# Hashed attention with a two-layer tail: later hashes and first maxima for three heads, and the maxima of a step ahead of the normalisation

## The chip, the cores and the metric

The program runs on one core of a Trainium2 chip. The metric is the device time of one execution in microseconds (us). Five engines work beside each other, each in its own order: TensorE (PE in the profile; its weight loads are PEld), VectorE (DVE), ScalarE (ACT), GpSimd (POOL) and SyncE (SP), whose queue issues most of the DMAs.

## The reference, cut to what matters

Attention with a hash mask, over 2 batches of 8 heads, 768 positions and 64 dimensions. A mixture-of-experts layer and a second two-layer network follow; the change touches only the attention.

```python
q_bits = (np.einsum('bhsd,dk->bhsk', q, proj) > 0)      # 6 bits: the bucket of a position
mask = q_bucket[:, :, :, None] == k_bucket[:, :, None, :]
scores = scale * np.matmul(q, k.transpose(0, 1, 3, 2))
scores = np.where(mask, scores, -1000000000.0)
scores = scores - np.max(scores, axis=-1, keepdims=True)
attn = np.exp(scores)
attn = attn / (np.sum(attn, axis=-1, keepdims=True) + 1e-09)
return np.matmul(attn, v)
```

## The kernel before

The 16 heads (batches laid end to end) are cut into 96 units of 128 keys, six to a head. The loop over `s` (line 950) issues one unit's scores in each step, and everything else at fixed offsets from it. The string `ORDER` (line 38) gives the order in which the parts of one step are issued; an engine runs its instructions in that order. The letters are:

- `a`, `b`: `ST(s, 0)` and `ST(s, 1)`, the scores of unit `s` against the two halves of the queries (two matmuls each, lines 861 and 862), and the exponential by ScalarE (L863).
- `V`: `vsplit(h, 0)`, ScalarE's scaled copy of a head's values (L755); its second half, two VectorE instructions (L759, L760), is issued at `o`.
- `D`: `flush()`, which issues the DMAs that the step before put off: hash rows into the operand slots (`op<-big`, L650), the slots' other parts (`op<-A`, `op<-B`, L650), loads, flags.
- `N`: `NORM(h)`, issued at steps 10, 16, 22 and so on: three VectorE instructions (L888 to L890) that read the accumulator `av` of head `h`.
- `m`, `n`: `MAX(u, 0)` and `MAX(u, 1)` for the units `us` of this step: a matmul of row block `u` of a head against half the keys (L829), and a VectorE maximum over it (L830). The hash rows must be in the slot before.
- `e`: `EL(s-1)`, the split of the exponentials into two float16 parts (L867 on ScalarE, L868 on GpSimd).
- `p`: `POSTa`, after the last unit of a head, joins the halves (L832). One step later `POSTb` is issued at `L`: a transpose on TensorE (L835), two VectorE instructions (L837, L841) and DMAs that put the maxima of the head into its slot (L838).
- `A`: in every second step `AV(s-5)` and `AV(s-4)`, 18 matmuls each into `av` (L876 to L878); for a head's last unit six more (L882). There is one `av` buffer, so a head's first `AV`, one step after `NORM`, must wait for `NORM` of the head before.
- `L`: `slot`, whatever `PLAN` (line 40) puts at the end of a step: `Z(...)`, hash matmuls (L802 to L804) with a threshold on VectorE (L809), `T(...)`, conversions and DMAs, `vscale` and `vscale2` (L734 to L749), `vtot`.

`ps5` gives `ST` and `MAX` five PSUM buffers in turn; all short work shares the two `misc` buffers. The first maxima (units 0 to 5) are taken ahead of the loop. How far the maxima run ahead is set by `us` (line 951): at most `cap[s]` units in step `s` (2 where the list has ended), and never past unit `s+10`. With the list of before, the maxima of head 2 (units 12 to 17) fall into steps 4, 4, 5, 5, 6 and 7, those of head 3 into steps 8 to 13, those of head 4 into steps 14 to 19. `Z3=(4,5)` puts the two halves of head 3's hash matmuls into steps 4 and 5.

Of the kernel before, what the change touches and what calls it, by code (L numbers as in the profile page):

```python
# [34 lines left out]
PB = 1  # L35
LAGS = (0, 0)
HB = 3
ORDER = "aVDNmbnefopAL"
PM = 2
PLAN = dict(  # L40
    v0=(1, 3, 4), T3=(2, 2), Z3=(4, 5), T=(2, 4, 5, 7), Z=(8, 10), ld=0, am1=(4, 6, 8, 9), am=(4, 6, 8,
    10), sc=(13, 15), tot=3, tot0=6, sp=(-2, 4, 10, 18), cap=(3, 2, 0, 1), x=(1, 2, 7, 3), x3=(0, 1, 2, 2), x4=(9, 10, 13, 11), w1=(91, 92, 95, 96, 97, 98, 99, 100), ga=(87, 88, 90), vl=1, am0=(0, 0), Z2=(0, 1), x6=(0, 1, 6, 4), first=(57, 58, 59, 60, 66, 72, 75, 78, 83, 84, 85, 86),
)
NPRE = 3
NT = 22
# [458 lines left out]
def _program(base, tc, nc, q, k, v, proj, mod, w_gate, mbias, w1, w2, win, wout, alpha, out):  # L504
# [445 lines left out]
    for s in range(96+LAG+2):  # L950
        us=[u for u in range(nu,min(96,s+6+LA+1,nu+(PLAN["cap"][s] if s<len(PLAN["cap"]) else 2)))]; nu+=len(us)
        fs=dq[:]; dq.clear()
        for o in "aVDNbmnefopAL" if s==0 else ORDER:
            t=s-1-LAG
# [613 lines left out]
```

## Time and profile before

| | us |
|---|---|
| median of three runs | 685.57 (683.86 to 687.6) |
| the profiled execution, its own time | 686.88 |
| its span, first to last instruction | 685.1 |
| PE busy | 656.4 (96%) |
| VectorE busy | 446.7 (65%) |
| ScalarE busy | 315.3 (46%) |
| GpSimd busy | 236.0 (34%) |

The span is that of the profiled execution, and all times of rows are counted from its start. The attention takes about the first 250 us. A matmul's record reaches to its modelled end, and matmuls overlap, so the idle time printed behind a row is a better guide to a wait than the busy share.

### The profile page before, as it was taken

Reading aid. Unit: us, or ns where it says so; the run is one execution under the profiler, and the core shown is the slowest. Engines: PE = TensorE matmul, PEld = TensorE weight load, DVE = VectorE, ACT = ScalarE, POOL = GpSimd, SP = SyncE. Lnnn points to the kernel's source line nnn. Section 1 sums busy time; section 2 is a strip of 40 time slices with the busy share of each in tenths; the row PEclk is TensorE's granted clock in tenths of the full one; section 3 lists DMA queues with packets and bytes.
Section 4 is the critical chain, followed back from the end, with each engine's and each line's share of the span. In section 5 each row is a group of like instructions: output and inputs, shape, how many; then the busy total and the mean of one; then the engine's idle time right before and its main releaser. Section 6 shows DMA issues by size and latency. Waiting matters only on the chain.

```text
span 685.1 us, 12778 instructions
## 1 busy us (share of the span) xinstructions
PE 656.4 (96%) x4938; PEld 556.2 (81%) x4938; DVE 446.7 (65%) x927; ACT 315.3 (46%) x536; POOL 236.0 (34%) x211
## 2 busy tenths in 40 slices
PE   7789999999999988999999999999999999999995
PEld 6578898998788878898888987888888888888884
DVE  6887878788888778455735668999443444433332
ACT  5567788887787843033423256665211111111111
POOL 8767999987967501310000202040030000200002
PEclk9979999999999999999999999999999999999998
DMA  8466864866603139385320834441020000100001
GB/s 217 129 146 142 187 154 97 185 185 138 140 11 125 49 107 395 119 321 201 108 61 11 285 120 154 131 146 62 1 93 1 15 16 0 47 16 0 1 0 61
DMA packets 32859, 75.02 MB, mean 110 GB/s; under 512 B 7276, under 2 KB 7366, under 8 KB 32534
## 3 DMA queue, kind: packets, MB, share of 16 engines
q1 hardware_dynamic: 29700, 64.43, 33.0%
q0 software_dynamic: 2960, 9.70, 4.3%
q8 instruction: 39, 0.64, 0.4%
q14 instruction: 30, 0.25, 0.1%
q10 hardware_dynamic: 130, 0.00, 0.0%
HBM read 49.79 MB, written 14.68 MB: 94 GB/s over the span
## 4 chain that ended last, share of the span: by engine, by line
PE 54%; DVE 1%; ACT 1%; issue 1%; POOL 1%; ACTq 0%; POOLq 0%
PE o L1413 19%; PE h L1387 18%; PE y L1074 8%; PE g L1054 8%; PE tr L1257 1%; POOL out_dram L1430 1%; PE tr L1041 0%; DVE w L1232 0%; DVE op L1232 0%; ACT op L1230 0%; DVE gl L620 0%; ACT gf L1391 0%; ACT q L1392 0%; ACT w L1230 0%; DVE big L1197 0%
## 5 line engine op out<-in xcount | busy, mean ns | idle before, releaser
L868 POOL TENSOR_TENSOR El<-E,Eh 128x768 f16<-128x768 f32 x87 | 142.7, 1652 | 36.6 <-ACT Eh L867 22.7
L863 ACT ACTIVATE E<-st 128x384 f32<-128x384 f32 x192 | 89.2, 494 | 53.3 <-PE st L862 49.8
L830 DVE TENSOR_REDUCE mx<-mxp 128x1 f32<-128x384 f32 x192 | 97.6, 548 | 9.2 <-PE mxp L829 8.7
L617 ACT ACTIVATE gh<-gf 128x512 fp32r<-128x512 f32 x48 | 30.3, 631 | 142.7 <-PE o L1413 132.2
L867 ACT ACTIVATE Eh<-E 128x768 f16<-128x768 f32 x94 | 79.8, 849 | 0.0
L861 PE MATMUL st<-op 97*128 97x384 f32 x192 | 72.9, 380 | 1.6 <-DMA op<-mr 1.3
L829 PE MATMUL mxp<-op 76*128 76x384 f32 x192 | 65.9, 357 | 7.3 <-ACT E L863 2.5
L620 DVE TENSOR_TENSOR gl<-gf,gh 128x512 fp32r<-128x512 f32 x48 | 33.1, 690 | 59.2 <-ACT gh L617 57.2
L1430 POOL DMA_INDIRECT out_dram<-x,did x12 | 11.8, 984 | 167.8 <-DVE x L1427 89.1
L1387 PE MATMUL h<-big,op 128*128 128x512 f32 x256 | 67.9, 393 | 0.0
L862 PE MATMUL st<-op 128*128 128x384 f32 x192 | 65.8, 343 | 0.0
L1413 PE MATMUL o<-op,gh 128*128 128x512 f32 x192 | 64.2, 395 | 0.0
L1245 POOL DMA_INDIRECT yg<-ys,dpos x10 | 12.3, 1231 | 138.3 <-DVE x L1197 72.8
L876 PE MATMUL av<-vh,Eh 128*128 128x65 f16 x576 | 58.5, 196 | 1.3 <-DVE big L890 1.3
L876 PEld LDWEIGHTS <-Eh 128*128 128x128 f16 x576 | 52.5, 98 | 8.4 <-issue 6.2
L1074 PE MATMUL y<-op,hh 128*128 128x512 f32 x172 | 58.6, 399 | 0.0
L877 PE MATMUL av<-vl,Eh 128*128 128x64 f16 x576 | 58.0, 194 | 0.0
L878 PE MATMUL av<-vh,El 128*128 128x65 f16 x576 | 57.8, 195 | 0.0
L1387 PEld LDWEIGHTS h<-big,op 128*128 128x128 f32 x256 | 48.1, 188 | 10.9
L877 PEld LDWEIGHTS <-Eh 128*128 128x128 f16 x576 | 53.2, 99 | 0.0
L878 PEld LDWEIGHTS <-El 128*128 128x128 f16 x576 | 53.1, 98 | 0.0
L1395 DVE TENSOR_SCALAR gf<-h,al 128x512 f32<-128x512 f32 x33 | 24.8, 751 | 41.7 <-PE h L1387 41.7
(424 smaller groups left out, 1483.2 us busy)
## 6 DMA issues: line engine op xcount, KB each, us to landing
r<-in_moe_w_dram SPq DMA_DIRECT2D x14, 1024.0 KB
op<-B SPq DMA_DIRECT2D x32, 192.0 KB
op<-A SPq DMA_DIRECT2D x28, 192.0 KB
op<-A SPq DMA_DIRECT2D x13, 384.0 KB
ys<-zero SPq DMA_DIRECT2D x19, 256.0 KB
op<-in_moe_w_in_dram SPq DMA_DIRECT2D x4, 1024.0 KB
op<-in_moe_w_out_dram SPq DMA_DIRECT2D x4, 1024.0 KB
ys<-ysb SPq DMA_DIRECT2D x13, 256.0 KB
```

Of the source, the lines that this page charges most:

```text
L829: mm(p[:,0:384],t[0:76,2,c*128:(c+1)*128],t[0:76,1,a*384:a*384+384],start=True,stop=True)
L830: nc.vector.tensor_reduce(out=mx[h][:,c,a:a+1],in_=p[:,0:384],axis=AX.X,op=ALU.max)
L861: mm(p[:,0:384],t[0:97,1,js],t[0:97,2,qs],start=True,stop=False)
L863: nc.scalar.activation(E[s][0][:,qs],p[:,0:384],AF.Exp,scale=0.125)
L867: else: nc.scalar.activation(eh,e,AF.Copy)
L868: (nc.vector if s>=ELD else nc.gpsimd).tensor_tensor(out=el,in0=e,in1=eh,op=ALU.subtract)
L876: mm(a[:,c*65:c*65+65],eh[:,cs],VH[h//4%2][:,j,h%4,:],start=(j==0 and c==0),stop=False,skip_group_check=True)
L877: mm(a[:,c*65:c*65+64],eh[:,cs],VL[h//4%2][:,j,h%4,:],start=False,stop=False,skip_group_check=True)
L878: mm(a[:,c*65:c*65+65],el[:,cs],VH[h//4%2][:,j,h%4,:],start=False,stop=False,skip_group_check=True)
L1074: nc.tensor.matmul(yps[key][i], a[:, ts], w[:, c], start=(c == 0 and m == 0), stop=(c == 7 and m == 2))
L1387: nc.tensor.matmul(p, terms[t][0][:, kk, cs], terms[t][1][:, kk], start=(n == 0), stop=(n == 11))
L1413: nc.tensor.matmul(po[b][i], a[:, ts], w[:, c % 2], start=(c == 0 and n == 0), stop=(c == 15 and n == 2))
```

## The change

Three settings. In `ORDER` the letter `N` moves from ahead of `m`, `b` to behind `n`: the three instructions of `NORM` are issued behind all maxima of their step. `Z3` becomes `(5,5)`: the first half of head 3's hash matmuls goes from step 4 to step 5. The list `cap` is longer and now sets the limits of steps 4 to 14 as well: the maxima of head 2 fall into steps 5, 5, 6, 6, 7 and 7, those of head 3 into steps 9, 9, 10, 11, 12 and 13, the first two of head 4 both into step 15; from there on all is as before. No instruction is added or taken away. Step 0 keeps an order of its own, written out in the loop.

```diff
-ORDER = "aVDNmbnefopAL"
+ORDER = "aVDmbnNefopAL"
 PLAN = dict(
-    v0=(1, 3, 4), T3=(2, 2), Z3=(4, 5), T=(2, 4, 5, 7), ...
-    10), sc=(13, 15), tot=3, tot0=6, sp=(-2, 4, 10, 18), cap=(3, 2, 0, 1), ...
+    v0=(1, 3, 4), T3=(2, 2), Z3=(5, 5), T=(2, 4, 5, 7), ...
+    10), sc=(13, 15), tot=3, tot0=6, sp=(-2, 4, 10, 18), cap=(3, 2, 0, 1, 0, 2, 2, 2, 0, 2, 1, 1, 1, 1, 0), ...
```

## Rows read from the trace of the kernel before

**Rows 1.** The page: PE's busy line; granted clock in 40 slices, tenths.
```profile
PE 656.4 (96%) x4938; PEld 556.2 (81%) x4938; DVE 446.7 (65%) x927; ACT 315.3 (46%) x536; POOL 236.0 (34%) x211
PEclk9979999999999999999999999999999999999998
```

**Rows 2.** Windows: stretch, length, busy us of each engine (instructions), granted clock, DMA share, GB/s.
```profile
30.00:50.00 20.00, 15.99 (x136) 13.06 (x135) 15.18 (x40) 12.72 (x24) 13.72 (x9) 0.74 0.51 119
50.00:160.00 110.00, 107.88 (x1495) 97.51 (x1494) 90.15 (x234) 88.44 (x164) 99.78 (x81) 1.00 0.70 163
```

**Rows 3.** Timeline of PE: start us, us, line, tile, count [idle before, releaser].
```profile
31.98 0.40 PE L747 MATMUL misc<-dg,one 128*128 128x4 f32 x2 [1.54 <-DVE dg L743]
...
33.88 0.98 PE L829 MATMUL mxp<-op 76*128 76x384 f32 x2 [0.66 <-ACT E L863]
...
38.08 0.37 PE L835 MATMUL misc<-ident,mt 128*6 128x128 f32 x1 [0.98 <-DVE vl L760]
```

**Rows 4.** Windows of one us where the granted clock falls and rises.
```profile
32.00:33.00 1.00, 1.00 (x4) 0.71 (x4) 0.97 (x4) 0.37 (x1) 1.00 (x1) 0.61 0.38 61
...
42.00:43.00 1.00, 1.00 (x21) 0.86 (x19) 0.00 (x0) 0.00 (x0) 1.00 (x1) 0.77 0.14 41
```

**Rows 5.** Timeline of SP's queue: hash rows of heads 2, 3, and 4 with 5.
```profile
30.67 1.55 SPq L650 DMA_DIRECT2D op<-big  x2
...
44.07 1.61 SPq L650 DMA_DIRECT2D op<-big  x2
...
59.85 3.14 SPq L650 DMA_DIRECT2D op<-big  x4
```

**Rows 6.** Timeline of PE: first maxima of head 3, step 9, first maxima of head 4.
```profile
48.28 0.41 PE L829 MATMUL mxp<-op 76*128 76x384 f32 x1 [0.83 <-ACT A L711]
...
49.10 0.42 PE L861 MATMUL st<-op 97*128 97x384 f32 x1
...
63.09 0.41 PE L829 MATMUL mxp<-op 76*128 76x384 f32 x1 [1.26 <-DMA op<-big]
```

**Rows 7.** Timeline of ACT, one row, and of DVE in steps 4 to 7.
```profile
33.64 0.58 ACT L755 ACTIVATE misc<-vr,sc 128x384 f32<-128x384 f32 x1
...
34.58 1.02 DVE L830 TENSOR_REDUCE mx<-mxp 128x1 f32<-128x384 f32 x2 [1.46 <-PE mxp L829]
...
37.38 0.56 DVE L760 TENSOR_TENSOR vl<-misc,vh 128x384 f16<-128x384 f32 x1
...
43.38 0.66 DVE L809 TENSOR_SCALAR big<-misc,tv 24x384 f32<-24x384 f32 x1 [1.63 <-PE misc L804]
...
47.87 0.15 DVE L832 TENSOR_REDUCE mt<-mx 128x6 f32<-128x12 f32 x1
```

**Rows 8.** Timeline of PE: the one wait of a head's first AV for NORM.
```profile
241.52 0.20 PE L876 MATMUL av<-vh,Eh 128*128 128x65 f16 x1 [1.27 <-DVE big L890]
```

**Rows 9.** Timelines of PE, then DVE: head 1's flags, next maxima, next AV, NORM.
```profile
66.24 0.36 PE L882 MATMUL av<-vt,fl 33*128 33x65 f16 x6
...
67.73 0.34 PE L829 MATMUL mxp<-op 76*128 76x384 f32 x1
...
69.11 0.21 PE L876 MATMUL av<-vh,Eh 128*128 128x65 f16 x1
...
67.02 0.21 DVE L888 TENSOR_SCALAR r<-av,sc 128x6 f32<-128x6 f32 x1
...
67.50 0.56 DVE L890 TENSOR_TENSOR big<-av,r 128x384 f32<-128x384 f32 x1
67.97 1.94 DVE L830 TENSOR_REDUCE mx<-mxp 128x1 f32<-128x384 f32 x4
```

**Rows 10.** The same for head 12, cut to the second maximum, the AV and NORM.
```profile
215.91 0.34 PE L829 MATMUL mxp<-op 76*128 76x384 f32 x1
...
217.35 0.21 PE L876 MATMUL av<-vh,Eh 128*128 128x65 f16 x1
...
215.03 0.23 DVE L888 TENSOR_SCALAR r<-av,sc 128x6 f32<-128x6 f32 x1 [0.71 <-PE av L882]
```

**Rows 11.** Timeline of PE: two later waits, for a DMA and for a maximum.
```profile
85.85 0.45 PE L861 MATMUL st<-op 97*128 97x384 f32 x1 [0.71 <-DMA op<-mr]
...
172.36 0.44 PE L829 MATMUL mxp<-op 76*128 76x384 f32 x1 [0.55 <-DVE mx L830]
```

More of the change, by code (lines that the diff above doesn't have):

```diff
@@ L37 @@
 HB = 3
-ORDER = "aVDNmbnefopAL"
+ORDER = "aVDmbnNefopAL"
 PM = 2
 PLAN = dict(
-    v0=(1, 3, 4), T3=(2, 2), Z3=(4, 5), T=(2, 4, 5, 7), Z=(8, 10), ld=0, am1=(4, 6, 8, 9), am=(4, 6, 8,
-    10), sc=(13, 15), tot=3, tot0=6, sp=(-2, 4, 10, 18), cap=(3, 2, 0, 1), x=(1, 2, 7, 3), x3=(0, 1, 2, 2), x4=(9, 10, 13, 11), w1=(91, 92, 95, 96, 97, 98, 99, 100), ga=(87, 88, 90), vl=1, am0=(0, 0), Z2=(0, 1), x6=(0, 1, 6, 4), first=(57, 58, 59, 60, 66, 72, 75, 78, 83, 84, 85, 86),
+    v0=(1, 3, 4), T3=(2, 2), Z3=(5, 5), T=(2, 4, 5, 7), Z=(8, 10), ld=0, am1=(4, 6, 8, 9), am=(4, 6, 8,
+    10), sc=(13, 15), tot=3, tot0=6, sp=(-2, 4, 10, 18), cap=(3, 2, 0, 1, 0, 2, 2, 2, 0, 2, 1, 1, 1, 1, 0), x=(1, 2, 7, 3), x3=(0, 1, 2, 2), x4=(9, 10, 13, 11), w1=(91, 92, 95, 96, 97, 98, 99, 100), ga=(87, 88, 90), vl=1, am0=(0, 0), Z2=(0, 1), x6=(0, 1, 6, 4), first=(57, 58, 59, 60, 66, 72, 75, 78, 83, 84, 85, 86),
 )
```

## The prediction

> **What bounds the kernel now.** I read the page first. PE is busy for 96% of the span, and its clock is lowest in the slice from 34 to 51 us [rows 1]. The change reaches only into the attention, so I took windows there. From 50 to 160 us PE is busy for 107.88 of 110 us: what is put on PE there, or makes it wait there, costs its full time. From 30 to 50 us it is another picture: PE 15.99 of 20, VectorE 15.18, the clock at 0.74 on average [rows 2]. Then the timeline of PE, reading only the idle time behind the rows. In steps 3 to 5 PE waits three times, 1.54, 0.66 and 0.98 us [rows 3]. The clock falls to 1.2 GHz right behind the first of these and is back at 2.4 GHz within the 43rd us: between the two lie some 10 us at half speed [rows 4]. PE had worked without a printed wait from 38.08 on when the clock rose. Two more waits stand in the change's way: 0.83 us ahead of head 3's first maximum (step 8) and 1.26 us ahead of head 4's (step 14) [rows 6].
>
> **Which of these waits the change touches.** The 1.54 us belong to step 3, where everything is issued as before; they stay, and so does the fall of the clock. The 0.66 us are put down to an exponential, but the buffer that this matmul takes (five back) held scores whose exponential was long over. What came just then are head 2's hash rows: their DMAs were issued until 32.22 [rows 5], and the matmul began 1.66 us later. Head 4's case gives the same delay: the second of four issues ends near 61.4 (half of 3.14 behind 59.85), and the matmul starts at 63.09. So this is a wait for hash rows, and one step more removes it. The 0.98 us are the wait of POSTb for a misc buffer that the value split holds until 37.94; the split stands on VectorE behind the four maxima of step 4 [rows 3, 7]. With these maxima and the first half of Z3 out of step 4, the split can start behind ScalarE's copy, at 34.25, and POSTb takes a buffer that is long free. Z3's first half goes to step 5, behind the AV matmuls, where PE does it anyway; SP's order doesn't change, since head 3's rows go out behind the second half, which stays in step 5.
>
> **Early part, placed by hand.** From 34.25 VectorE has, up to the last maximum of head 2 and its POSTa: the value splits of heads 0 and 1 (1.05 each, from the 0.56 of a row), 12 maxima (0.48 each: a pair ends after 1.02, and the rows overlap a little), two thresholds of 0.6, two absolute maxima of 0.46 and about 1 us of small ones: 2.1 + 5.8 + 1.2 + 0.9 + 1.0 = 11.0 us. It can't be through before 45.2. In the trace of before this same work ends at 48.02, because VectorE stands idle for 1.46, 1.63 us and less [rows 7]. With PE's own order laid beside it (scores of step 4 from 32.2, POSTb, step 5's scores and four maxima, AV, the six hash matmuls), VectorE waits another 0.8 us for hash and maximum matmuls if the clock is back soon, and 2.7 us if it stays low until 42.4: POSTa ends at 46.0 or at 47.9. PE is then ahead: it has done step 8's scores by 44.3 (or 46.5) and its transpose in POSTb waits for POSTa. Step 9 starts right behind, at 46.05 or 47.95 instead of 49.10 [rows 6]; it carries two more maximum matmuls than before (0.36 us). So the early part is worth 2.7 us at one end and 0.8 at the other. I take the middle, 1.8, because the rows show both an unbroken stretch of about 3.6 us behind 32.2 and a short new wait at its end (the last maximum of step 5 needs a buffer that an exponential frees near 36.5). The 0.83 us wait is inside this sum.
>
> By the Trainium skill, TensorE: Matmul & The Clock Gate, section Terms, the loss at a reduced clock is the reduced time multiplied by the missing share of the clock. By that rule the 10 us would cost 5 us, more than the whole early part gives in my sum. No row shows PE alone there; VectorE's 15.18 of 20 us [rows 2] speak against it.
>
> **Head 4's wait.** SP's hash rows for head 4 stand in a queue that runs nearly without a break from 44.07 to 63 [rows 5], and this queue starts when head 3's second threshold is through, 44.04 [rows 7], in my placement near 39.8 to 41.7. The rows land two to four us earlier, PE comes about 1.8 us earlier, and the maximum comes one step later. All of the 1.26 us goes [rows 6]. Together: 1.8 + 1.26 = 3.1 us gained.
>
> **NORM behind the maxima.** A head's first AV must wait for NORM; once before, 1.27 us [rows 8]. In heads 0 to 13 NORM is through 0.9 to 2.1 us ahead of that AV (1.05 in head 1, [rows 9]). Now two maxima (0.95 us) go ahead, and more than that where VectorE would first stand idle for the matmul of the second maximum. Head 1: the flags' matmuls have given VectorE its work at 66.24 to 66.6, NORM starts at 67.02 and ends at 68.06, AV starts at 69.11. In the new order VectorE waits for the matmul that ends at 68.07, takes that maximum from 68.12, NORM from 68.6 to 69.62: AV is late by 0.56 [rows 9]. Head 12 in the same way: matmul end 216.25, NORM 216.8 to 217.8, AV late by 0.50 instead of waiting for nothing [rows 10]. Doing this for all 13 heads that have maxima in that step gives 0.56, 0.49, 0.57, 0.26, 0.37, 0.20 and 0.50 for heads 1, 3, 5, 7, 9, 11 and 12, and 0.26 to 0.36 to spare in heads 0, 2, 4, 6, 8 and 10, which have the hash matmuls or other work between. Sum 2.95 us, on the engine that is full. Some of it can hide in later waits that don't hang on PE: head 1's 0.56 in the 0.71 us for a DMA at 85.85 [rows 11]. I take 2.4. The bounds are 3.0, or more if VectorE runs later than now (a rival), and below nothing by 0.55, since the maxima of that step come 1 us earlier and one wait for a maximum is on record [rows 11], though not in such a step.
>
> **Sum.** -1.8 - 1.26 + 2.4 = -0.7 us on the profiled execution (686.88, span 685.1), so 686.2 there. The three runs have their median 1.3 us lower, at 685.57; the forecast is 684.9. A measurement of this kernel can tell about 0.5%, 3.4 us, from no change.
>
> **Rivals.** First: the clock comes back early and PE, not VectorE, limits the early part. Then the two waits (1.64) and half of some 6.5 us at half speed (3.2) come back in full: -1.64 - 3.2 - 1.26 + 2.4 = -3.7, 681.9. For it: VectorE's idle time is of the same size. Against it: the 11.0 us of VectorE work. 0.13. By the Trainium skill's rule above the early part would go this way.
>
> Second: NORM costs nothing, because later waits like the two of [rows 11] take up the stalls (ten between 85 and 240 us, 0.2 to 0.7 each): -3.1, 682.5, or 681.0 with the early end of the first part. For it: those waits are there; against: most of the stalls lie before 160, where PE has hardly one. 0.17.
>
> Third, the slow side: VectorE is later at those steps than I place it. The point that decides is 0.3 us: from there the six heads with 0.26 to 0.36 to spare stall too. At 0.45 us later all heads lose 2.95 + 7 x 0.45 + 6 x 0.15 = 7.0 us, less 3.1: +3.9, 689.5. For it: the waits in the early part go, so PE comes to VectorE's queue sooner. Against: VectorE is busy for 90 of 110 us there [rows 2]. 0.10.
>
> **How the numbers follow.** The forecast with its bounds (gain 2.1 to 4.0, NORM -0.5 to 3.0: -4.5 to +0.9) has 0.60. The range of 681.0 to 688.6 leaves out the far end of the slow rival and the two gains added up. Faster by over 0.5% (below 682.1): the first rival, half of the second: 0.21. Slower by over 0.5% (above 689.0): most of the third: 0.08. The rest, 0.71, is no change that can be told.
>
> **What would show it.** Right: no wait at the first maxima of heads 2, 3 and 4 nor at step 4's POSTb; a new wait of PE for POSTa at step 8; step 9 starting between 46 and 48; waits of 0.2 to 0.6 us for NORM at odd heads. Wrong: a PE wait of more than 0.8 us for NORM at many heads, no such wait at any, or a second stretch at half clock near 46, which the new wait could bring on and which I have left out of the sum.

## The result: slower by 0.77%

The changed kernel takes 690.22 us in the median of seven runs (690.07 to 692.38), the kernel before 685.88 (683.86 to 687.6): a ratio of 1.0077, 95% interval 1.0059 to 1.0095. The forecast was 684.9 with a range of 681.0 to 688.6, and a chance of 0.08 that the change would cost more than 0.5%. The profiled execution took 692.38 us, its span is 690.6.

The page of the changed kernel, PE's busy line and the clock as in [rows 1]:

```profile
PE 657.6 (95%) x4938; PEld 558.4 (81%) x4938; DVE 447.5 (65%) x927; ACT 316.0 (46%) x536; POOL 236.3 (34%) x211
PEclk9998999999999989999999999999999999999999
```

The work is the same on every engine to within 1.2 us (the weight loads to within 2.2); what is new is waiting, and two slices of lower clock at other places than before. From the timeline of PE in the changed kernel, from step 3 to the end of the attention: its waits above 1.1 us, and one of its five AV waits for `NORM`:

```profile
30.34 0.39 PE L747 MATMUL misc<-dg,one 128*128 128x4 f32 x2 [1.54 <-DVE dg L743]
34.49 0.44 PE L829 MATMUL mxp<-op 76*128 76x384 f32 x1 [1.14 <-ACT E L863]
38.57 0.42 PE L861 MATMUL st<-op 97*128 97x384 f32 x1 [1.49 <-DMA op<-mr]
45.42 0.27 PE L835 MATMUL misc<-ident,mt 128*6 128x128 f32 x1 [1.40 <-DVE mt L832]
61.72 0.44 PE L829 MATMUL mxp<-op 76*128 76x384 f32 x1 [1.15 <-ACT E L863]
95.43 0.20 PE L876 MATMUL av<-vh,Eh 128*128 128x65 f16 x1 [0.63 <-DVE big L890]
...
148.85 0.73 PE L182 MATMUL misc<-ident,big 128*128 128x128 f32 x3 [1.71 <-DVE big L890]
...
245.50 0.24 PE L876 MATMUL av<-vh,Eh 128*128 128x65 f16 x1 [1.26 <-DVE big L890]
```

Step 3 is reached 1.64 us earlier than in before (30.34 against 31.98): nothing is changed ahead of it, but the clock had not fallen near 12 us in this execution (the granted clock from 12 to 13 us is 1.00, in before 0.50). So places are compared by intervals, from one head's flags' matmuls (L882) to the next. They are the start times of those rows, subtracted; the first interval begins at the L747 row of step 3.

| interval, us | before | changed | order alone | maxima alone | late at 52 only | not at 52 |
|---|---|---|---|---|---|---|
| step 3 to head 3 | 61.08 | 61.74 | 59.97 | 60.13 | 60.52 | 60.47 |
| head 3 to 7 | 52.41 | 53.46 | 53.49 | 52.43 | 52.42 | 53.48 |
| head 7 to 8 | 13.88 | 17.23 | 15.68 | 13.85 | 18.63 | 13.85 |
| head 8 to 14 | 77.21 | 77.78 | 78.17 | 77.21 | 76.78 | 78.10 |
| head 14 to 15 | 9.73 | 12.43 | 9.73 | 9.73 | 9.73 | 11.31 |

For the two profiles alone: +0.66 to head 3, +1.05 to head 7, +3.35 between heads 7 and 8, +0.57, and +2.70 in the last interval, 8.3 us; 1.64 of it was saved ahead of step 3 and 1.2 behind the attention, which leaves the 5.5 us between the spans. The +2.70 doesn't follow the change: a wait of 1.27 us stands there in before too, and the clock fell behind it in the changed kernel's execution and not in that of before. Seven of the fourteen profiles of this study have this interval at 11.0 to 12.5 us, the other seven at 9.7: five of the nine with a late normalisation, two of the five without. The +3.35 does, as the next section shows.

Over whole executions the clock is no lower than before: its mean is 0.987 in the seven runs of the changed kernel, and 0.987 in the 23 to 29 runs of the kernel before in each of the first three series below. So the change brought no more half speed in sum; its loss is waiting.

### The profile page after: what moved, and what is told of

Read it like the earlier page. It is cut to its first block, busy times and chain, and to the rows that moved or that the text cites. A ratio compares the mean times of both kernels' runs of the same rounds, so it can differ in the third digit from the quotient of the medians.

```text
span 690.6 us, 12781 instructions
## 1 busy us (share of the span) xinstructions
PE 657.6 (95%) x4938; PEld 558.4 (81%) x4938; DVE 447.5 (65%) x927; ACT 316.0 (46%) x536; POOL 236.3 (34%) x211
## 4 chain that ended last, share of the span: by engine, by line
PE 54%; DVE 1%; ACT 1%; issue 1%; POOL 1%; ACTq 0%; POOLq 0%
PE o L1413 18%; PE h L1387 18%; PE y L1074 8%; PE g L1054 8%; PE tr L1257 1%; POOL out_dram L1430 1%; PE tr L1041 0%; DVE w L1232 0%; DVE op L1232 0%; ACT op L1230 0%; DVE gl L620 0%; ACT gf L1391 0%; ACT q L1392 0%; ACT w L1230 0%; DVE big L1197 0%
## 5 line engine op out<-in xcount | busy, mean ns | idle before, releaser
L876 PE MATMUL av<-vh,Eh 128*128 128x65 f16 x576 | 60.9, 199 | 4.1 <-DVE big L890 4.1
L876 PEld LDWEIGHTS <-Eh 128*128 128x128 f16 x576 | 53.9, 100 | 11.9 <-DVE big L890 6.2
L877 PE MATMUL av<-vl,Eh 128*128 128x64 f16 x576 | 60.4, 197 | 0.0
L878 PE MATMUL av<-vh,El 128*128 128x65 f16 x576 | 60.1, 198 | 0.0
L877 PEld LDWEIGHTS <-Eh 128*128 128x128 f16 x576 | 54.6, 101 | 0.1
L878 PEld LDWEIGHTS <-El 128*128 128x128 f16 x576 | 54.5, 100 | 0.0
```

Of the source, the lines that this page charges most:

```text
L876: mm(a[:,c*65:c*65+65],eh[:,cs],VH[h//4%2][:,j,h%4,:],start=(j==0 and c==0),stop=False,skip_group_check=True)
L877: mm(a[:,c*65:c*65+64],eh[:,cs],VL[h//4%2][:,j,h%4,:],start=False,stop=False,skip_group_check=True)
L878: mm(a[:,c*65:c*65+65],el[:,cs],VH[h//4%2][:,j,h%4,:],start=False,stop=False,skip_group_check=True)
```

## What happens at step 52

In step 52 the normalisation of head 7 ends a batch. At the end of that step the router transposes the column block that heads 6 and 7 have written (L182, issued by `hook`). The timeline of DVE in the changed kernel there:

```profile
146.65 1.08 DVE L830 TENSOR_REDUCE mx<-mxp 128x1 f32<-128x384 f32 x2 [1.42 <-PE mxp L829]
147.75 0.22 DVE L888 TENSOR_SCALAR r<-av,sc 128x6 f32<-128x6 f32 x1
148.01 0.19 DVE L889 RECIPROCAL r<-r 128x6 f32<-128x6 f32 x1
148.24 0.56 DVE L890 TENSOR_TENSOR big<-av,r 128x384 f32<-128x384 f32 x1
```

VectorE stands idle for 1.42 us, though the flags' matmuls of head 7 are done at 145.89: it waits for the first maximum's matmul, takes both maxima and only then the normalisation. The row of 148.85 above starts right at its end. In before, the same three instructions began at 145.86 and were over at 146.91, 0.06 us ahead of the transposes, where the AV that follows had 1.51 us to spare:

```profile
145.86 0.23 DVE L888 TENSOR_SCALAR r<-av,sc 128x6 f32<-128x6 f32 x1 [0.70 <-PE av L882]
...
146.35 0.56 DVE L890 TENSOR_TENSOR big<-av,r 128x384 f32<-128x384 f32 x1
...
146.97 0.55 PE L182 MATMUL misc<-ident,big 128*128 128x128 f32 x3
```

Windows of the changed kernel around it (columns as in [rows 2]):

```profile
148.00:149.00 1.00, 0.15 (x1) 0.15 (x2) 0.95 (x3) 0.64 (x1) 1.00 (x1) 1.00 0.00 0
149.00:150.00 1.00, 1.00 (x5) 1.00 (x5) 0.97 (x3) 0.00 (x0) 1.00 (x2) 0.54 0.46 197
152.00:153.00 1.00, 1.00 (x29) 1.00 (x27) 0.10 (x1) 1.00 (x2) 0.43 (x1) 0.75 1.21 492
```

Behind the wait the clock is at 1.2 GHz until within the 153rd us. The granted clock of the four windows from 149 to 153 is 0.54, 0.50, 0.50 and 0.75, some 3.4 us at half speed. With the order alone (below) the same wait stands there without a fall of the clock, and the interval is longer by 1.80 us; so of the 3.35 us here 1.80 come from the wait and 1.55 from the half speed. By the Trainium skill, TensorE: Matmul & The Clock Gate, section Terms, the loss at a reduced clock is the reduced time multiplied by the missing share of the clock, which gives an estimate of 1.7 us for 3.4 us at half speed. The trace's 1.55 us agrees with it here, where PE has no other wait.

## The experiments

Theory A: the late normalisation carries the loss, above all by readers other than the AV matmuls, and the moved maxima are worth nothing because the waits they remove come back as others. Rivals: the normalisation costs the 2.4 us of the prediction and the moved maxima the rest (B), or the clock does (it falls once more near 64 us in the changed kernel). All were timed beside the kernel before.

**The order alone.**

```diff
-ORDER = "aVDNmbnefopAL"
+ORDER = "aVDmbnNefopAL"
```

> Only the order of the letters is changed, as in the changed kernel; Z3 and cap are those of before. Theory A: the late normalisation carries the loss. In the trace of the changed kernel PE waits 1.71 us for it at step 52, where the router's transposes read its output in the same step, runs some 3.4 us at half clock behind that, and waits 0.4 to 0.7 us ahead of the AV of five heads. Sum 1.7 + 1.7 + 2.8 = 6 us: some 691 to 692. Rival B, the prediction's own price of 2.4 us: 688.3, and then the moved maxima carry the rest.

Measured: 689.38 us, before 686.08; ratio 1.0068 (1.0041 to 1.0094). The rows of PE with idle time that the order brought:

```profile
67.19 0.20 PE L876 MATMUL av<-vh,Eh 128*128 128x65 f16 x1 [0.56 <-DVE big L890]
93.86 0.20 PE L876 MATMUL av<-vh,Eh 128*128 128x65 f16 x1 [0.64 <-DVE big L890]
120.87 0.20 PE L876 MATMUL av<-vh,Eh 128*128 128x65 f16 x1 [0.55 <-DVE big L890]
147.33 0.55 PE L182 MATMUL misc<-ident,big 128*128 128x128 f32 x3 [1.71 <-DVE big L890]
...
177.57 0.20 PE L876 MATMUL av<-vh,Eh 128*128 128x65 f16 x1 [0.41 <-DVE big L890]
...
205.20 0.20 PE L876 MATMUL av<-vh,Eh 128*128 128x65 f16 x1 [0.71 <-DVE big L890]
218.65 0.20 PE L876 MATMUL av<-vh,Eh 128*128 128x65 f16 x1 [0.51 <-DVE big L890]
```

Six AV waits of 3.38 us in sum and the 1.71 us for the transposes. Behind the latter the clock didn't fall in this execution:

```profile
147.00:148.00 1.00, 0.67 (x5) 0.68 (x6) 0.97 (x3) 0.12 (x1) 1.00 (x1) 1.00 0.00 0
148.00:149.00 1.00, 1.00 (x13) 0.84 (x12) 1.00 (x3) 0.67 (x2) 1.00 (x2) 1.00 0.93 393
```

So the same wait of 1.71 us is followed by half speed in one execution (interval 17.23) and not in another (15.68). The order alone is about as slow as the whole change. It is less slow than the 691 to 692 expected: the mean granted clock of its six executions is 0.988, no lower than in before, and later waits take up part of the AV waits (from head 8 to 14 the interval is longer by 0.96 us for 1.63 us of waits).

**The maxima and Z3 alone.**

```diff
-ORDER = "aVDmbnNefopAL"
+ORDER = "aVDNmbnefopAL"   # cap and Z3 as in the changed kernel
```

> The moved maxima and Z3 as in the changed kernel, the normalisation at its old place. Theory A: the waits removed (0.66, 0.98, 0.83, 1.26 us) come back as others (in the changed kernel 1.14 at step 5, 1.49 for a DMA at step 6, 1.40 at step 8, 1.15 at step 15), so 685 to 687, no change. The prediction's sum for this part: 3.1 us faster, 682.8. Rival B: the moved maxima bring the clock down a second time near 64 us and cost 2 to 3 us: 688 to 689.

Measured: 684.56 us, before 686.08; ratio 0.9991 (0.9977 to 1.0004). No difference can be told from zero, and no cost: B falls. Waits of PE in the early part of this run:

```profile
34.40 0.45 PE L829 MATMUL mxp<-op 76*128 76x384 f32 x1 [1.14 <-ACT E L863]
38.41 0.41 PE L861 MATMUL st<-op 97*128 97x384 f32 x1 [1.42 <-DMA op<-mr]
45.25 0.27 PE L835 MATMUL misc<-ident,mt 128*6 128x128 f32 x1 [1.36 <-DVE mt L832]
61.56 0.44 PE L829 MATMUL mxp<-op 76*128 76x384 f32 x1 [1.15 <-ACT E L863]
```

Four waits of 5.07 us in place of four of 3.73 (0.66, 0.98, 0.83, 1.26). Two of them are the same thing: in a step with two units the sixth PSUM buffer asked for is the one of that step's own first scores, and their exponential is late on ScalarE. The third is the DMA of head 1's maxima, queued on SP behind five large ones (VectorE is done with these maxima at 33.93, SP issues their DMA at 35.13). From step 3 to head 3 the run takes 60.13 us against 61.08.

**The changed kernel with step 52 in the old order.**

```diff
-        for o in "aVDNbmnefopAL" if s==0 else ORDER:
+        for o in "aVDNbmnefopAL" if s==0 else "aVDNmbnefopAL" if s==52 else ORDER:
```

> The changed kernel, but in step 52 alone the normalisation of head 7 stands ahead of the maxima again. Theory A: the wait of 1.71 us for the transposes and the half clock behind it go, 3.3 us: 686.9. If the stretch at half clock near 149 us was chance and not brought on by this wait: 1.7 us, 688.5. If other waits take its place: 690.

Measured: 688.14 us, ratio 1.0030 (1.0015 to 1.0044) where the whole change has 1.0077: one step out of 96 is worth 0.47%, 3.2 us, by the ratios and 2.1 us by the medians. The intervals of the two ratios leave some 1.6 to 4.8 us, so this run doesn't tell the two first expectations apart, the wait with its half speed (3.3 us) or without (1.7). The interval from head 7 to 8 is 13.85 us again.

**The changed kernel with head 4's maxima back in step 14.**

```diff
-cap=(3, 2, 0, 1, 0, 2, 2, 2, 0, 2, 1, 1, 1, 1, 0)
+cap=(3, 2, 0, 1, 0, 2, 2, 2, 0, 2, 1, 1, 1, 1)
```

> The changed kernel, but the first maxima of head 4 are back in step 14, one unit a step. Theory A: the wait of 1.26 us for hash rows doesn't return in full, because the queue of DMAs is some 4 us earlier by now, and the wait of 1.15 us at step 15 for an exponential goes: 689 to 690, up to 1 us faster than the changed kernel. The prediction's view: the move was worth 1.26 us, so undoing it gives 691.5. Rival B: the four maxima of step 15 bring the clock down near 64 us, and undoing them gives 3 us: 687.

Measured: 688.84 us, ratio 1.0053 (1.0033 to 1.0074). Its interval overlaps that of the whole change, so a gain of about 1.4 us is likely and not certain. In its profile the 1.15 us wait is gone, one of 0.61 us for a maximum stands near 61.6, and no wait for hash rows: with the DMAs earlier, these rows were there in step 14 as well. Undoing the move did not cost the 1.26 us that the prediction had booked for it.

**Before, with the normalisation late in step 52 only.**

```diff
+        for o in "aVDNbmnefopAL" if s==0 else "aVDmbnNefopAL" if s==52 else ORDER:   # ORDER as in before
```

> The kernel before, but in step 52 alone the normalisation of head 7 stands behind the maxima. Theory A: the router's three transposes at the end of that step wait 1.7 us for it, and in some executions the clock falls behind the wait (1.7 us more): 1.7 to 3.4 us slower than before, 687.8 to 689.4, and the AV of head 8's first unit waits for nothing. The prediction's own account of that step, a late AV by 0.26: 686.3.

Measured: 688.46 us, before 685.63; ratio 1.0044 (1.0028 to 1.0061), 2.8 to 3.0 us from moving three instructions behind two in one step. The wait and the clock there:

```profile
146.86 0.90 PE L182 MATMUL misc<-ident,big 128*128 128x128 f32 x3 [1.71 <-DVE big L890]
```
```profile
148.00:150.00 2.00, 2.00 (x15) 1.69 (x14) 1.60 (x4) 1.09 (x3) 1.42 (x2) 0.50 0.95 393
150.00:152.00 2.00, 2.00 (x34) 2.00 (x32) 0.28 (x1) 1.35 (x2) 1.24 (x1) 0.50 1.00 369
```

The interval is 18.63 us here: the half speed began within the wait (the granted clock from 146 to 147 us is 0.78) and lasted some 6.8 us, where it was 3.4 in the changed kernel.

**Before, with the normalisation late everywhere but in step 52.**

```diff
+ORDER = "aVDmbnNefopAL"
+        for o in "aVDNbmnefopAL" if s==0 else "aVDNmbnefopAL" if s==52 else ORDER:
```

> The kernel before with the new order of letters in every step but 52. The prediction's price for the late normalisation holds for what is left: waits ahead of the AV of heads 2, 4, 6, 10, 12 and 13 of 0.4 to 0.7 us, 2.4 to 3.4 us in sum, 688.5 to 689.4. If later waits took them up: 686.1, as before.

Measured: 688.12 us, before 685.63; ratio 1.0034 (1.0020 to 1.0047), 2.3 to 2.5 us. The AV waits in its profile are those of the order alone (0.55, 0.64, 0.55, 0.41, 0.71, 0.51, 3.37 us in sum). The term of the prediction was 2.4 us, and its size holds. With the 2.8 us of step 52 the two parts make 5.3, the order alone 3.3 to 4.7 by median and ratio.

**The router's transposes a step later.**

```diff
+ORDER = "aVDmbnNefopAL"
-x3=(0, 1, 2, 2)
+x3=(1, 1, 2, 2)
```

> The new order of letters in every step, maxima and Z3 as before, but the first transposes of the router's fourth column block are issued at the end of step 53 instead of 52, so that the normalisation may be late. Theory A: the wait of 1.71 us is gone without touching the order, and the AV waits stay: 688.5 to 689.4, like the run with step 52 left out. If the loss at step 52 came from something else than this reader: as the run with the new order alone, 689.4 to 691.

Measured: 690.24 us, before 685.63; ratio 1.0071 (1.0053 to 1.0089). The 1.71 us wait is gone, and nothing is gained: theory A in this form failed. PE's rows with idle time, and SP's queue from the normalisation of head 7 on:

```profile
148.81 0.20 PE L876 MATMUL av<-vh,Eh 128*128 128x65 f16 x1 [0.64 <-DVE big L890]
...
167.23 0.45 PE L861 MATMUL st<-op 97*128 97x384 f32 x1 [1.13 <-DMA op<-mr]
```
```profile
148.78 0.35 SPq L892 DMA_DIRECT2D x_d<-big  x1
149.23 4.80 SPq L650 DMA_DIRECT2D op<-A  x3
...
162.39 0.76 SPq L838 DMA_DIRECT2D op<-mr  x1
```

The same queue in before, where head 7's flags' matmuls start at the same time, 145.47:

```profile
146.94 0.35 SPq L892 DMA_DIRECT2D x_d<-big  x1
147.39 3.52 SPq L650 DMA_DIRECT2D op<-A  x3
...
160.70 0.76 SPq L838 DMA_DIRECT2D op<-mr  x1
```

Two more instructions wait for `NORM(7)`. The AV behind it waits 0.64 us, hidden until now under the transposes' wait. And the write of the batch to DRAM (L892) is issued by SP right behind the normalisation: it goes out 1.84 us later, everything behind it in the queue with it, down to the maxima of head 9, 1.69 us later, for which PE now waits 1.13 us, in before 0.54 (with the order alone it was 0.45). Theory C: this write is a third path of the loss.

**That write put off to the end of the next step's DMAs.** The two settings of the run above, and:

```diff
-            nc.sync.dma_start(out=x_d[...], in_=xs[b])
+            f=lambda:nc.sync.dma_start(out=x_d[...], in_=xs[b])
+            f() if b else later(f,3)
```

> As the run with the router's transposes a step later (new order of letters), and the write of the first batch's normalised output to DRAM, which SP issues right behind the normalisation of head 7, is put off to the end of the next step's DMAs. Theory C: this write is a third reader; SP's queue stood behind it for 1.84 us longer than in before (3.31 instead of 1.47 us behind the flags' matmuls), and the wait of 1.13 us for the maxima's DMA at 167 us (0.54 in before) came from that. It should fall to 0.5 us or less, head 9's interval from 15.1 to 14.5, the AV wait of 0.64 stay: 0.6 us less than that run, some 689.2 to 689.6 (+0.5 to +0.6% on before). If the wait came from something else, it stays at 1.1 and the time at 690.

Measured: 688.34 us, before 685.60; ratio 1.0042 (1.0027 to 1.0058), where the run without it has 1.0071. The wait at 167 us is gone altogether, the interval from head 8 to 9 falls from 15.11 to 14.06 us (14.49 in before), the AV wait of 0.63 stays. C holds for the wait. The time is below the 689.2 to 689.6 expected: the gain of the medians, 1.9 us, is larger than the 1.05 us that this interval shows. The rest isn't explained by a row, and the intervals of the two ratios overlap a little.

**Half of the move.**

```diff
-ORDER = "aVDNmbnefopAL"
+ORDER = "aVDmNbnefopAL"
```

> The kernel before with the normalisation behind the first maximum of its step instead of ahead of it: half of the move. If its lateness is what costs, it is now late by one maximum and by the wait for that one's matmul, some 0.95 us less than in the new order: the AV waits of 0.4 to 0.7 us go altogether, and the transposes' wait at step 52 falls from 1.71 to some 0.7 us. Then 686.2 to 686.8, at most 1 us slower than before. If the loss doesn't follow the lateness: 688 to 690.

Measured: 686.91 us, before 685.80; ratio 1.0019 (1.0004 to 1.0035). PE's waits for the normalisation in its profile:

```profile
147.98 0.55 PE L182 MATMUL misc<-ident,big 128*128 128x128 f32 x3 [1.18 <-DVE big L890]
...
205.32 0.20 PE L876 MATMUL av<-vh,Eh 128*128 128x65 f16 x1 [0.24 <-DVE big L890]
```

Five of six AV waits are gone and the sixth has shrunk by 0.47 us; the transposes' wait has shrunk by 0.53, not by 1.0 as expected. Behind the start of the flags' matmuls head 7's normalisation is over after 2.73 us here, after 3.26 with the order alone and after 1.44 in before. The loss follows the lateness: 1.1 to 1.3 us (by median and by ratio) for one maximum, 3.3 to 4.7 for two.

**The wait in step 3 filled.** Ten matmuls on constants (20 instructions) ahead of the one that waits, in before and in the run with the maxima of heads 2 and 3 moved:

```diff
-sl_at(PLAN["v0"][1],lambda:vscale2(0))
+sl_at(3,lambda:idle(10)); sl_at(PLAN["v0"][1],lambda:vscale2(0))
```

> The kernel before, with ten matmuls on constants (20 instructions, some 1.4 us at full clock, into a buffer nobody reads) ahead of the one that waits 1.54 us in step 3. PE isn't idle there any more, so the clock should stay at 2.4 GHz through steps 4 to 8, where it was at 1.2 GHz for some 10 us in the trace of before. If that stretch costs what the early part's VectorE work leaves over (heads' first interval 18.1 us at full clock in the run with the moved maxima alone, 19.5 in before): 1.0 to 1.9 us faster, 683.8 to 684.6. If half the slow time comes back in full: 5 us, 680.6. If VectorE sets the pace there whatever the clock is: no change, 685.6.

> The same ten matmuls in the kernel with the old order of letters, Z3 and the maxima of heads 2 and 3 moved, head 4's not. Its profile had the clock at half speed there too. If the two gains add: 0.9 us from the moved maxima and 1.0 to 1.9 from the clock, 683.0 to 683.8. If the moved maxima gain only because they sometimes keep the clock up: as the run with the filled wait alone.

Measured: 686.42 us against 685.80, ratio 1.0006 (0.9995 to 1.0016), and 686.54, ratio 1.0008 (0.9994 to 1.0022). Neither gains. PE's timeline and windows of the first:

```profile
35.88 0.27 PE L835 MATMUL misc<-ident,mt 128*6 128x128 f32 x1 [1.80 <-DVE vl L760]
60.03 0.41 PE L829 MATMUL mxp<-op 76*128 76x384 f32 x1 [1.59 <-DMA op<-big]
83.00 0.45 PE L861 MATMUL st<-op 97*128 97x384 f32 x1 [0.91 <-DMA op<-mr]
```
```profile
36.00:38.00 2.00, 2.00 (x9) 1.74 (x8) 2.00 (x6) 0.85 (x2) 1.98 (x2) 0.66 0.63 135
84.00:86.00 2.00, 2.00 (x10) 1.69 (x10) 1.49 (x3) 1.98 (x5) 0.50 (x1) 0.60 0.33 54
```

PE has no wait in step 3 any more; it waits 1.80 instead of 0.98 us for VectorE at step 4's POSTb, and the clock falls behind that. From step 3 to head 0 it is 2.3 us less (17.15 against 19.46), and by head 3 they are gone (60.85 against 61.08). The interval from head 0 to 1 is longer by 0.35 us, with a wait for hash rows of 1.59 instead of 1.26; the one from head 2 to 3 by 1.73 us, with a wait for a DMA of 0.91 instead of 0.71 and a second stretch of some 3.4 us at half speed behind it. So the filling didn't keep the clock up, it moved the half speed: the mean granted clock of its eleven executions is 0.989, in before 0.987. What the early part takes with the clock up is read from the moved maxima, in the part on the clock below. In the second run the clock stayed up until 47 us and then fell for some 3.4 us, behind a wait of 1.39 us for POSTa at 45.50.

**The old order with the maxima of heads 2 and 3 moved, head 4's not.**

```diff
-cap=(3, 2, 0, 1)
+cap=(3, 2, 0, 1, 0, 2, 2, 2, 0, 2, 1, 1, 1, 1)   # Z3=(5, 5)
```

> The old order of letters, Z3 and the maxima of heads 2 and 3 moved, those of head 4 as before. Theory A: the 1.15 us wait for an exponential at step 15 goes, and the 1.26 us wait for hash rows at step 14 comes back smaller (some 0.6, since VectorE and the queue of DMAs are earlier): 683.5 to 684.5, faster than before by 0.2 to 0.4%. If the move of head 4's maxima was the useful part: 685.7.

Measured: 684.72 us, before 685.63; ratio 0.9993 (0.9979 to 1.0006). As with head 4's moved: no difference. No kernel of this study beats the one of before by more than the measurement can tell.

## Why the prediction was wrong, point by point

**The step that failed** is the first sentence under "NORM behind the maxima": "A head's first AV must wait for NORM". That is one instruction that waits, and the whole working looked at it alone, for all 13 heads. For the normalisation of head 7 two more wait: the transposes of the router in the same step, which `hook` issues and which I did not look up, and the write to DRAM, behind which SP's queue stands. Head 7 was booked with 0.26 us. Made late alone, it costs 2.8 to 3.0 us: 1.71 us of waiting and half speed with it in some executions. The write goes out 1.84 us later, and that shows as a longer wait of PE (1.13 us, in before 0.54) once the transposes are moved out of the way.

**A second term failed, by as much: the gain of the early part, 1.8 + 1.26 us, did not come.** It is 0.6 us by the ratio of the run with the maxima alone, with zero inside its interval. Head 7 with 2.5 to 2.7 us more than booked and this with 2.5 us less make up the distance of 5.0 to 6.0 us between the forecast and the result. The waits named for head 2, POSTb, head 3 and head 4 did go. What the placement lacked: the DMA of head 1's maxima (1.42 us), which SP issues behind head 3's five large ones, and the buffer wait at step 15 (1.15). Its twin at step 5 I had foreseen as a short wait (it was 1.14), and not seen that two units in step 15 make the same pattern. POSTa's wait at step 8 came as placed (1.36). Up to step 9 the placement is near: it begins 15.1 us behind the L747 row in the changed kernel and 17.1 in before, 2.0 us earlier, where 1.15 to 3.05 were placed.

**The AV waits were placed well, and the sum came out with some luck.** Foretold for heads 1, 3, 5, 9, 11 and 12: 0.56, 0.49, 0.57, 0.37, 0.20 and 0.50; in the run with the order alone 0.56, 0.64, 0.55, 0.41, 0.71 and 0.51. Head 11 was off by 0.5. The six heads with 0.26 to 0.36 us to spare did not wait, so the slow rival, lateness at all heads, did not come. Head 1's 0.56 us went into the 0.71 us wait at 85.85, as foretold: that wait is absent with the order alone. The term, 2.4 us, is what the run without step 52 costs (2.3 to 2.5); but the waits of these six heads are 3.4 us there and not 2.7, and more of them hides than the 0.55 us allowed.

**The clock.** "They stay, and so does the fall of the clock" was wrong: the 1.54 us wait is in every profile without filling, but the fall behind it isn't. In the changed kernel and with the maxima alone the clock stayed up and fell near 63 us instead, behind the 1.15 us wait of step 15; with step 52 in the old order it fell in the 41st us. The first rival, that with the clock back two waits and 3.2 us return, is refuted by these profiles. Five kernels with moved maxima and no filling are the same up to head 0's flags' matmuls. From step 3 to there it is 18.13 us in the changed kernel and 18.06 with the maxima alone, where the clock stayed up, and 19.39 without head 4's move, where it was at half speed for some 10.2 us, as in before (19.46). The other two, with some 6.8 us at half speed, lie at 18.64 and 19.80. So the clock's return is worth some 1.3 us there. The Trainium skill's rule (TensorE: Matmul & The Clock Gate, section Terms), by which 10.2 us at half speed would cost an estimated 5.1, agrees behind step 52 and not here, where PE waits for others: with the clock up the waits of 1.14 and 1.42 us stand in this stretch, and without head 4's move, at half speed, only 0.21 us is left of them.

**The bounds.** The second rival's 681.0 "with the early end of the first part" is 681.6 by its own terms (2.7 + 1.26 us). The sign of a second stretch at half clock near 46 us came in one profile, that of the moved maxima with the filled wait.

**What is open.** How much of step 52's cost is half speed on average. The profiles show it in two of five with that wait at 1.71 or 1.18 us. An estimate from the mean granted clocks: 0.985 in the eight executions of the run with step 52 late, 0.987 in the 25 of before beside it, which is 1.7 us more of missing clock (the span times the missing share). Among the executions of before, in the three largest series, a run with 1 us more of missing clock takes some 0.5 us longer, so some 0.9 of the 2.8 to 3.0 us would be half speed. The six executions with the order alone show no more missing clock than before, so this isn't settled.

## What to carry to other kernels

When an instruction is moved later, list everything that waits for it: every reader of what it writes, every next user of what it releases, in helpers and hooks too, and every queue that stands behind such a wait. Take the tightest one, not the usual one: here it had 0.06 us to spare and the usual one 1.51. One exceptional step out of 96 was 2.8 to 3.0 us of a loss of 4.3 to 5.3. And where a wait is removed in a stretch that three engines and a DMA queue pace together, look for the next wait in the same step before booking the gain: here 3.7 us of waits went and 5.1 came.

## What the runs showed of the hardware that was not expected

The same wait of PE, 1.71 us, goes with a fall to 1.2 GHz in some executions (behind it in the changed kernel, from within it in the run late at 52 only) and not in others (order alone, head 4 back). The wait of 1.27 us near 241 us is followed by it in seven profiles of fourteen. The intervals with the fall are 1.3 to 3.0 us longer than those without (11.0 to 12.5 against 9.7; 17.23 and 18.63 against 15.68). So the profile of a single execution can put up to 2.7 us into an interval where the change has nothing to do, and a difference of that size between two profiles needs a count over several before it is read as an effect.
